# GpSimd's last two column sums wait for VectorE, the sum over rows moves to other PSUM banks, and a split moves ahead of two small steps

## The chip, the cores and the metric

The kernel runs on one core of a Trainium2 chip. A core has TensorE (PE in the profile: matmuls; PEld: its weight loads), VectorE (DVE), ScalarE (ACT), GpSimd (POOL) and SyncE (SP, which issues most DMAs). The metric is the device time of one execution in microseconds; three executions of the kernel before took 457.15, 457.48 and 458.14 us, so the time before is the median, 457.48 us.

## The reference

```python
x = A_x                                    # (1, 2048, 512)
g = sigmoid((x * gate_w).sum(-1, keepdims=True))
# a: linear attention, 32 heads of 16
q, k, v = split_heads(x @ wqkv)
pq, pk = q @ w_phi, k @ w_phi              # per head, 16 x 16
phi_q = concat(softmax(pq), softmax(-pq)); phi_k = concat(softmax(pk), softmax(-pk))
kv = phi_k^T v;  z = phi_k.sum over rows
o  = (phi_q kv) / (phi_q . z + 1e-6)
a  = merge_heads(o) @ wo
# b: dense, Mish, dense (512 -> 1376 -> 512)
h = x @ w1 + b1;  b = (h * tanh(softplus(h))) @ w2
return g * a + (1 - g) * b
```

All data is fp32. Matmuls are made of three passes over a rounded high part and a low part of each operand (high x high, high x low, low x high), so most operands have a pair of tiles, h and l, and a step that makes the low part by a subtraction.

## The kernel before, in words

**Stage A** goes over the rows in eight chunks of 256 (two tiles of 128 rows each). For a chunk, TensorE projects k, v and q; the q projection is written to DRAM (`pqd`) for later. For each k tile VectorE makes the arguments of both softmaxes (steps `mx`, `mn`, `d0`, `d1`), ScalarE takes the exponential in place (`E`), VectorE sums per head, inverts and scales (`S`, `rS`, `ml`), TensorE adds phi_k^T v into one PSUM bank (`kv`), and GpSimd adds the tile into `zacc`, 128 x 1024 (`z0`, `z1`, L318). Beside that the weights of b are loaded and split.

**The seam** is the last chunk (the text `LAST`, L55 to 58) and the start of block 0. It also starts block 0: it splits block 0's x into `xbh` (`XH0`, `XH1`, ScalarE) and `xbl` (`XL0`, `XL1`, VectorE, L403), and takes the feature steps of block 0's first two q tiles (names with `+`, which mean the next stage). `zacc` is split into `zs` high (`zh`, ScalarE, L443) and low (`zl`, VectorE, L466), and TensorE multiplies both with a matrix of ones (`z`, L457 to 463), so that every row of `zb` holds the sum over all rows. `km` masks the kv sums, `kt` transposes them into `kvb`.

**Stage B** goes over the rows in four blocks of 512. TensorE works on the dense part: `up0` to `up10` (12 matmuls each, in the order xbh x w1 high, xbh x w1 low, xbl x w1 high), ScalarE takes Mish and makes the high part (`mi`, `hi`), GpSimd the low part (`lo`, L498), and `dn` adds into four PSUM banks (the four row tiles). Between these lie the attention steps: for each of the block's four q tiles, feature steps as above, then the product with `zb` (`T`), its sums (`D`), the denominator (`m`, `de`, `rd`, `sc`), the scaled features (`es`), a 32 x 32 transpose (`tr`); for each pair of tiles 16 DMAs that rearrange the transposed features (`mv`, `tt` into `eT`, L586), the numerator on TensorE (`nu`, 32 matmuls), its split (`oh` on ScalarE, `ol` on VectorE, L607), and the output projection (`wo`, 12 matmuls a tile) with its gated copy (`ag`). `fi` mixes both and stores.

**What sets the order.** Each engine runs its instructions in the order in which the program emits them: `pin` is `tc.keep_in_program_order`, and nearly every instruction is pinned to the one before it on its engine. The order is written out by hand in the texts `FIRST` to `BLOCK` (L39 to 86): words are steps, registered with `at` and called by `run`; a step with `@` in front is one of `mid_ops`, `'` means the previous chunk and `+` the next one. Waits between engines follow from the tiles that are read, written or reused. In `LAST`, before the change, z0 stands ahead of ve0 and of the feature steps of block 0's second q tile; in `BLOCK0`, the row `S1+ T1+ rS1+ D1+ LX0 LX1 nu1 oh1 ol1` puts the reciprocal and the sums of the next block's second tile ahead of ol1 on VectorE. LX0 and LX1 load the next block's x.

PSUM has eight banks: tag `a` has three (projections, `up`, kvT, z, half of num and wo), `dn` four (v, `down`), `kv` one.

The listing has the functions that the diff touches, with the line numbers of the profile.

Of the kernel before, what the change touches and what calls it, by code (L numbers as in the profile page):

```python
# [10 lines left out]
F32R = mybir.dt.float32r  # L11
AF = mybir.ActivationFunctionType
# [3 lines left out]
P = 128  # L16
S = 2048
D = 512
H = 32
DH = 16  # L20
KT = D // P
NG = 4
SC = 256
NCH = S // SC
# [28 lines left out]
    S1 rS1 ml1 z1 v1 ve1 q0 mx0+ mn0+ d00+ d10+ qe0 st0 q1 qe1 st1 E0+ lq1+  # L53
"""
LAST = """  # L55
    k0 mx0 mn0 d00 d10 k1 E0 XH0 kv' mx1 mn1 d01 d11 E1 v0 S0 rS0 ml0 z0 ve0 ldo XH1 mx1+ mn1+ d01+ d11+ E1+
    S1 rS1 ml1 z1 XL0 XL1 v1 ve1 lq2+ q0 WH0 qe0 st0 q1 WH1 zh qe1 st1 zl kv S0+ rS0+ km
"""


# [4 lines left out]
    up4 mi4 hi4 lo4 dn2 E2 S2 T2 rS2 D2 m2 de2 rd2 sc2 es2 tr2 up5 mi5 hi5 lo5 dn3 E3 ge gg up6 mi6 hi6 lo6 dn4  # L65
    up7 mi7 hi7 lo7 dn5 nu0 oh0 S3 T3 rS3 ol0 D3 m3 de3 rd3 sc3 es3 tr3 mv1 up8 mi8 hi8 lo8 dn6
    mx0+ mn0+ d00+ d10+ mx1+ mn1+ d01+ d11+ lq2+ lq3+ wo0 ag0 wo1 ag1 E0+ E1+ S0+ T0+ rS0+ D0+ m0+ de0+ rd0+ sc0+ es0+ tr0+
    up9 mi9 hi9 lo9 dn7 up10 mi10 hi10 lo10 dn8 S1+ T1+ rS1+ D1+ LX0 LX1 nu1 oh1 ol1 m1+ de1+ rd1+ sc1+ es1+ tr1+ mv0+
    XH0+ XL0+ XH1+ XL1+ dn9 wo2 ag2 wo3 ag3 df0 fi0 df1 fi1 df2 fi2 df3 fi3
"""  # L70
BLOCK1 = """
# [18 lines left out]
def tile_gated_mix(ctx: ExitStack, tc: tile.TileContext, xT, wv, wkT, wqT, bd, w1a, w1b, b1, w2a, w2b, wo, out):  # L90
# [6 lines left out]
    pin = tc.keep_in_program_order  # L97
    V, G_, A_, Sy = nc.vector, nc.gpsimd, nc.scalar, nc.sync
# [11 lines left out]
    def k4(name, tag, dt=F32):  # L110
        return T([P, 1024], dt, tag, {"E": 4, "tx": 2, "oh": 2, "z": 1}[tag], name)
# [4 lines left out]
    def psum(name, tag, bufs={"a": 3, "dn": 4, "kv": 1}):  # L116
        nm[0] += 1
        return pp.tile([P, 512], F32, name=f"{name}_{nm[0]}", tag=tag, bufs=bufs[tag])

    def act(out_, in_, fn=AF.Copy, **k):  # L120
        return pin(A_.activation(out_, in_, fn, **k))  # L121

    def kt(t, f):
        return t[:, : KT * f].rearrange("p (k f) -> p k f", f=f)

    def hv(ap):
        return ap.rearrange("p (h f) -> p h f", f=DH)

    def f32(ap):
        return ap.bitcast(F32)  # L130
# [5 lines left out]
    def stage(wT):  # L136
        return T([P, NFA * 512], F32, "w1a", 2, "wT")[:, : KT * 512].rearrange("p (k g f) -> p k g f", k=KT, f=P)

    skT, sqT = stage(wkT), stage(wqT)
    bds = k2("bds", "io")[:, :].rearrange("p (g f) -> p g f", g=NG)  # L140
    pin(A_.dma_start(bds, bd))
# [28 lines left out]
    ps = psum("warm", "dn")  # L170
# [25 lines left out]
    def at(key, name, fn):  # L196
        steps.setdefault((key, name), []).append(fn)
# [12 lines left out]
    zacc = k4("zacc", "z")  # L210
# [39 lines left out]
    def feat_ops(key, t, src, d):  # L250

        n = str(t)

        def red(name, op):
            d[name] = T([P, H], F32, name, 2, name)
            pin(V.tensor_reduce(d[name], hv(src()), axis=AX.X, op=op))  # L256

        def dd(a):
            if "E" not in d:
                d["E"] = k4("E", "E")  # L260
            E = hv(d["E"][:, a * 512 : (a + 1) * 512])
            if a == 0:
                pin(V.tensor_sub(E, hv(src()), d["mx"][:, :, None].to_broadcast([P, H, DH])))
            else:
                pin(V.tensor_sub(E, d["mn"][:, :, None].to_broadcast([P, H, DH]), hv(src())))  # L265

        def ss():
            d["S"] = T([P, 2 * H], F32, "Sm", 2, "Sm")
            pin(V.tensor_reduce(d["S"], hv(d["E"][:, :]), axis=AX.X, op=ALU.add))  # L269

        at(key, "mx" + n, lambda: red("mx", ALU.max))
        at(key, "mn" + n, lambda: red("mn", ALU.min))
        at(key, "d0" + n, lambda: dd(0))
        at(key, "d1" + n, lambda: dd(1))
        at(key, "E" + n, lambda: act(d["E"], d["E"], AF.Exp))
        at(key, "S" + n, ss)
        at(key, "rS" + n, lambda: pin(V.reciprocal(d["S"], d["S"])))  # L277
# [4 lines left out]
    def a_ops(c):  # L282
        key = ("A", c)
        P_ = psA[c] = {}
        for t in range(2):
            d = {}
            Es[c, t] = d

            def k_(t=t):
                P_["k", t] = proj(xs[c], t, wkh, wkl, "a")  # L290

            def v_(t=t):
                P_["v", t] = proj(xs[c], t, wvh, wvl, "dn" if c or t else "kv")

            def q_(t=t):
                P_["q", t] = proj(xs[c], t, wqh, wql, "a")

            def ve(t=t):
                vs[c, t] = k2("v", "io")
                act(vs[c, t], P_["v", t])  # L300

            def qe(t=t):
                P_["qs", t] = k2("qs", "pq")
                act(P_["qs", t], P_["q", t])

            def st(t=t):
                i = 2 * c + t
                pin(Sy.dma_start(pqd[i * P : (i + 1) * P, :], P_["qs", t]))

            at(key, f"k{t}", k_)  # L310
            at(key, f"v{t}", v_)
            at(key, f"q{t}", q_)
            at(key, f"ve{t}", ve)
            at(key, f"qe{t}", qe)
            at(key, f"st{t}", st)
            feat_ops(key, t, lambda t=t: P_["k", t][:, :], d)
            at(key, f"ml{t}", lambda d=d: scale_by(d, V))
            at(key, f"z{t}", lambda d=d: pin(G_.tensor_add(zacc, zacc, d["E"])))  # L318

        def kv():  # L320
            if not kvs:
                kvs.append(psum("kvp", "kv")[:, : NG * 64].rearrange("p (g f) -> p g f", g=NG))
            (kvp,) = kvs
            for t in range(2):
                E, v = Es[c, t]["E"], vs[c, t]
                Ev = E[:, :].rearrange("p (a r b x) -> p b r a x", a=2, r=2, b=8)
                for u in range(8):
                    for r in range(2):
                        o = (u % 2) * 64 + 32 * r
                        mm(kvp[o : o + 32, u // 2, :], v[:, u * 64 + 32 * r : u * 64 + 32 * r + 32], Ev[:, u, r, :, :],  # L330
                           start=(c == 0 and t == 0 and u < 2), stop=(c == NCH - 1 and t == 1), skip_group_check=True)

        at(key, "kv", kv)
        if c + 1 < NCH:
            def xh():
                new_x(c + 1)
                for j in range(2):
                    x_hi(c + 1, j)

            at(key, "xh", xh)  # L340
            for j in range(2):
                at(key, "xl", lambda j=j: x_lo(c + 1, j, G_))
        if c + 2 < NCH:
            at(key, "ldx", lambda: ldx(c + 2))
# [40 lines left out]
    xb = {}  # L385
    wob = {}

    def x_ops(b, load, split):

        raw = {}  # L390
        for h in range(2):
            def ld(h=h):
                raw[h] = k4("xraw", "tx")
                pin(Sy.dma_start(kt(raw[h], SC), xT[2 * b + h]))

            def xh(h=h):
                if b not in xb:
                    xb[b] = kt(k8("xbh", "xbh"), RB), kt(k8("xbl", "xbl"), RB)
                act(xb[b][0][:, :, h * SC : (h + 1) * SC], kt(raw[h], SC))

            def xl(h=h):
                sl = slice(h * SC, (h + 1) * SC)
                pin(V.tensor_sub(xb[b][1][:, :, sl], kt(raw[h], SC), f32(xb[b][0][:, :, sl])))  # L403

            at(load[0], load[1 + h], ld)
            at(split, f"XH{h}", xh)
            at(split, f"XL{h}", xl)
# [28 lines left out]
    B = {}  # L436

    def mid_ops():
        key = ("A", NCH - 1)

        def zh():
            B["zs"] = [k4("zs", "tx", F32R) for _ in range(2)]
            act(B["zs"][0], zacc)  # L443

        def km():
            B["km"] = k2("km", "io")
            shape = [P, NG, 2, 64]
            m = mask[:, :, :, :].rearrange("p r a f -> p r (a f)")[:, None, :, :].to_broadcast(shape)
            pin(V.tensor_mul(B["km"][:, :].rearrange("p (g r f) -> p g r f", g=NG, r=2), kvs[0][:, :, None, :].to_broadcast(shape), m))

        def kt_():
            pt = psum("kvT", "a")
            for G in range(NG):
                pin(nc.tensor.transpose(pt[:, G * P : (G + 1) * P], B["km"][:, G * P : (G + 1) * P], ident))
            act(kvb, pt[:, :].rearrange("p (g d) -> p g d", g=NG))

        def z():  # L457
            B["zb"] = k4("zb", "z")
            for a in range(2):
                ps = psum("z", "a")  # L460
                for j in range(2):
                    mm(ps, onr, B["zs"][j][:, a * 512 : (a + 1) * 512], start=(j == 0), stop=(j == 1))
                act(B["zb"][:, a * 512 : (a + 1) * 512], ps)

        at(key, "zh", zh)
        at(key, "zl", lambda: pin(V.tensor_sub(B["zs"][1], zacc, f32(B["zs"][0]))))  # L466
        at(key, "km", km)
        at(("B", 0), "@kt", kt_)
        at(("B", 0), "@z", z)


# [302 lines left out]
```

## Time and profile before

| | |
|---|---|
| runs | 457.15, 457.48 (median), 458.14 us |
| profiled execution, first to last instruction (span) | 455.6 us |
| profiled execution, own device time | not given apart from its span |
| granted TensorE clock | 0.998 of full speed |

The profile is of one execution. Its timeline has, per row, the start and the duration in us, the engine, the line, the operation, and output tile <- input tiles with partitions x elements; `x4` means that four such instructions are merged into the row. What stands in brackets is how long the engine stood idle before it, and what released it. L101 and L121 are the helpers through which all matmuls and all activations go, so these are told apart by their tiles. In the view of waits a row has the waiting engine, tile and line, whom it waited for, and then total us, number of waits and the longest. The chain of waits is followed back from the last instruction; its rows have start, duration and what ran. SPq is SyncE's DMA queue.

### The profile page before, as it was taken

Reading aid. Unit: us, or ns where it says so; the run is one execution under the profiler, and the core shown is the slowest. Engines: PE = TensorE matmul, PEld = TensorE weight load, DVE = VectorE, ACT = ScalarE, POOL = GpSimd, SP = SyncE. Lnnn points to the kernel's source line nnn. Section 1 sums busy time; section 2 is a strip of 40 time slices with the busy share of each in tenths; the row PEclk is TensorE's granted clock in tenths of the full one; section 3 lists DMA queues with packets and bytes.
Section 4 is the critical chain, followed back from the end, with each engine's and each line's share of the span. In section 5 each row is a group of like instructions: output and inputs, shape, how many; then the busy total and the mean of one; then the engine's idle time right before and its main releaser. Section 6 shows DMA issues by size and latency. Waiting matters only on the chain.

```text
span 455.6 us, 6980 instructions
## 1 busy us (share of the span) xinstructions
PE 445.6 (98%) x2772; PEld 363.4 (80%) x2772; DVE 306.8 (67%) x402; ACT 195.0 (43%) x265; POOL 161.4 (35%) x102
## 2 busy tenths in 40 slices
PE   7999999999999899999899999999999999999996
PEld 6888888888888678878687887887887888787885
DVE  2599459369399999799987985666967629611002
ACT  3554443443334645726337354434254553234220
POOL 3338777767862355221123212023212122221211
PEclk9999999999999999999999999999999999999999
DMA  7721513505523110313434050332041402030002
GB/s 284 247 83 56 168 53 129 186 8 179 183 82 106 47 23 2 94 46 86 146 94 138 17 158 14 108 115 54 23 119 53 112 19 94 1 81 13 1 1 92
DMA packets 25593, 40.07 MB, mean 88 GB/s; under 512 B 5716, under 2 KB 13908, under 8 KB 25560
## 3 DMA queue, kind: packets, MB, share of 16 engines
q1 hardware_dynamic: 25384, 39.35, 28.4%
q8 instruction: 22, 0.36, 0.3%
q10 hardware_dynamic: 144, 0.26, 0.2%
q14 instruction: 11, 0.09, 0.1%
q0 software_dynamic: 32, 0.01, 0.0%
HBM read 22.82 MB, written 8.40 MB: 69 GB/s over the span
## 4 chain that ended last, share of the span: by engine, by line
PE 61%; DVE 4%; ACT 1%; issue 0%
PE up L101 25%; PE down L101 24%; PE wo L101 10%; PE num L101 2%; DVE xbl L403 1%; DVE Sm L269 1%; DVE T L548 0%; DVE Dn L552 0%; DVE io L633 0%; ACT L121 0%; DVE tt L566 0%; DVE E L280 0%; DVE Dn L572 0%; ACT E L121 0%; DVE Sm L277 0%; ACT io L121 0%
## 5 line engine op out<-in xcount | busy, mean ns | idle before, releaser
L498 POOL TENSOR_TENSOR l<-act,h 128x512 fp32r<-128x512 f32 x44 | 60.7, 1380 | 224.2 <-ACT h L121 189.4
L121 ACT ACTIVATE act<-up,b1s 128x512 f32<-128x512 f32 x44 | 30.3, 689 | 91.5 <-PE up L101 90.3
L318 POOL TENSOR_TENSOR zacc<-zacc,E 128x1024 f32<-128x1024 f32 x16 | 39.7, 2482 | 45.8 <-DVE E L280 31.4
L121 ACT ACTIVATE E<-E 128x1024 f32<-128x1024 f32 x32 | 33.6, 1059 | 49.4 <-DVE E L265 49.4
L280 DVE TENSOR_TENSOR E<-E,Sm 128x1024 f32<-128x1024 f32 x32 | 44.0, 1375 | 1.1
L101 PE MATMUL wo<-woh,ohl 128*128 128x512 f32 x128 | 40.8, 390 | 1.2 <-DVE ohl L607 1.2
L269 DVE TENSOR_REDUCE Sm<-E 128x64 f32<-128x1024 f32 x32 | 38.7, 1209 | 3.8 <-ACT E L121 3.8
L101 PE MATMUL down<-w2ah,h 128*128 128x512 f32 x96 | 37.5, 390 | 0.0
L101 PE MATMUL down<-w2al,h 128*128 128x512 f32 x96 | 37.4, 389 | 0.0
L101 PE MATMUL down<-w2ah,l 128*128 128x512 f32 x96 | 37.4, 389 | 0.0
L633 DVE SCALAR_TENSOR_TENSOR io<-down,og_sb,io 128x512 f32<-128x512 f32 x16 | 11.3, 751 | 31.1 <-PE down L101 31.0
L256 DVE TENSOR_REDUCE mx<-proj 128x32 f32<-128x512 f32 x16 | 11.0, 689 | 30.8 <-PE proj L101 30.8
L101 PE MATMUL down<-w2bh,h 128*128 128x512 f32 x80 | 31.2, 391 | 0.0
L101 PE MATMUL down<-w2bl,h 128*128 128x512 f32 x80 | 31.1, 389 | 0.0
L101 PE MATMUL down<-w2bh,l 128*128 128x512 f32 x80 | 31.1, 389 | 0.0
L101 PEld LDWEIGHTS wo<-woh,ohl 128*128 128x128 f32 x128 | 24.0, 188 | 6.6 <-DVE ohl L607 1.6
L121 ACT ACT_TABLE_LOAD x19 | 24.4, 1283 | 10.1 <-PE up L101 9.8
L121 ACT ACTIVATE h<-act 128x512 fp32r<-128x512 f32 x44 | 27.8, 632 | 1.4
L607 DVE TENSOR_TENSOR ohl<-num,ohl 128x512 fp32r<-128x512 f32 x16 | 10.2, 678 | 26.4 <-ACT ohl L121 26.4
L101 PE MATMUL up<-xbl,w1ah 128*128 128x512 f32 x96 | 25.8, 391 | 1.5 <-DVE xbl L403 1.5
L101 PE MATMUL up<-xbh,w1ah 128*128 128x512 f32 x96 | 26.3, 396 | 0.2 <-ACT zb L121 0.2
L101 PE MATMUL up<-xbh,w1al 128*128 128x512 f32 x96 | 25.7, 389 | 0.0
(113 smaller groups left out, 970.6 us busy)
## 6 DMA issues: line engine op xcount, KB each, us to landing
xraw<-in_xT_dram SPq DMA_DIRECT2D x16, 512.0 KB, 4.8
eT<-tt SPq DMA_DIRECT2D x128, 64.0 KB, 2.0
pqd<-qs SPq DMA_DIRECT2D x16, 256.0 KB, 3.5
pq<-pqd SPq DMA_DIRECT2D x16, 256.0 KB, 2.8
out_dram<-io SPq DMA_DIRECT2D x16, 256.0 KB, 2.1
raw<-in_w1a_dram SPq DMA_DIRECT2D x3, 512.0 KB, 3.6
raw<-in_w2a_dram SPq DMA_DIRECT2D x3, 512.0 KB, 3.7
wT<-in_wkT_dram SPq DMA_DIRECT2D x4, 256.0 KB, 5.4
```

What stands on the lines that cost most here:

```text
L101: return pin(nc.tensor.matmul(*a, **k))
L121: return pin(A_.activation(out_, in_, fn, **k))
L256: pin(V.tensor_reduce(d[name], hv(src()), axis=AX.X, op=op))
L269: pin(V.tensor_reduce(d["S"], hv(d["E"][:, :]), axis=AX.X, op=ALU.add))
L280: pin(eng.tensor_mul(hv(d["E"][:, :]), hv(d["E"][:, :]), d["S"][:, :, None].to_broadcast([P, 2 * H, DH])))
L318: at(key, f"z{t}", lambda d=d: pin(G_.tensor_add(zacc, zacc, d["E"])))
L403: pin(V.tensor_sub(xb[b][1][:, :, sl], kt(raw[h], SC), f32(xb[b][0][:, :, sl])))
L498: pin(G_.tensor_sub(U[i]["l"], U[i]["a"], f32(U[i]["h"])))
L607: pin(V.tensor_sub(ohl[h, gp][:, 512:], num[h, gp], f32(ohl[h, gp][:, :512])))
L633: pin(V.scalar_tensor_tensor(io[t], dn[t], og_sb[:, i : i + 1], io[t], op0=ALU.mult, op1=ALU.add))
```

## The change

1. In `LAST`, z0 moves behind `d11+` and z1 behind `XL1`. The first GpSimd instruction of each also gets a hand-made dependency: z0 on the subtraction of d11+, z1 on that of XL1 (`last[0]` and `last[1]`). z1 is made of two halves of 512 columns.
2. `zh` and `zl` are in halves as well (`zh0 zl0 zh1 zl1`), and stand at the end of `LAST`, behind `km`.
3. A step `tb` asks for the activation table of Mish, behind `qe1 st1`. It isn't pinned.
4. z's two PSUM tiles are taken from tag `dn` instead of `a`.
5. In `BLOCK0`, `nu1 oh1 ol1` move ahead of `rS1+ D1+ LX0 LX1`.

```diff
 LAST
-    k0 mx0 mn0 d00 d10 k1 E0 XH0 kv' mx1 mn1 d01 d11 E1 v0 S0 rS0 ml0 z0 ve0 ldo XH1 mx1+ mn1+ d01+ d11+ E1+
-    S1 rS1 ml1 z1 XL0 XL1 v1 ve1 lq2+ q0 WH0 qe0 st0 q1 WH1 zh qe1 st1 zl kv S0+ rS0+ km
+    k0 mx0 mn0 d00 d10 k1 E0 XH0 kv' mx1 mn1 d01 d11 E1 v0 S0 rS0 ml0 ve0 ldo XH1 mx1+ mn1+ d01+ d11+ z0 E1+
+    S1 rS1 ml1 XL0 XL1 z1 v1 ve1 lq2+ q0 WH0 qe0 st0 q1 WH1 qe1 st1 tb kv S0+ rS0+ km zh0 zl0 zh1 zl1
 BLOCK0
-    up9 mi9 hi9 lo9 dn7 up10 mi10 hi10 lo10 dn8 S1+ T1+ rS1+ D1+ LX0 LX1 nu1 oh1 ol1 m1+ de1+ rd1+ sc1+ es1+ tr1+ mv0+
+    up9 mi9 hi9 lo9 dn7 up10 mi10 hi10 lo10 dn8 S1+ T1+ nu1 oh1 ol1 rS1+ D1+ LX0 LX1 m1+ de1+ rd1+ sc1+ es1+ tr1+ mv0+
...
+    SYNC = mybir.DependencyInfo(mybir.DependencyClass.Sync, mybir.DependencyReason.DATA)
+    last = {}
...
-                pin(V.tensor_sub(E, d["mn"][:, :, None].to_broadcast([P, H, DH]), hv(src())))
+                ins = pin(V.tensor_sub(E, d["mn"][:, :, None].to_broadcast([P, H, DH]), hv(src())))
+                if key == ("B", 0) and t == 1:
+                    last[0] = ins
...
-            at(key, f"z{t}", lambda d=d: pin(G_.tensor_add(zacc, zacc, d["E"])))
+            def zs(t=t, d=d):
+                for a in range(2 if c == NCH - 1 and t else 1):
+                    sl = slice(a * 512, a * 512 + 512) if c == NCH - 1 and t else slice(0, 1024)
+                    ins = pin(G_.tensor_add(zacc[:, sl], zacc[:, sl], d["E"][:, sl]))
+                    if c == NCH - 1 and not a:
+                        tc.add_manual_dep(ins.ins, last[t].ins.name, SYNC, reason="VectorE's own sums first")
+            at(key, f"z{t}", zs)
...
-                pin(V.tensor_sub(xb[b][1][:, :, sl], kt(raw[h], SC), f32(xb[b][0][:, :, sl])))
+                last[h] = pin(V.tensor_sub(xb[b][1][:, :, sl], kt(raw[h], SC), f32(xb[b][0][:, :, sl])))
...
-        def zh():
-            B["zs"] = [k4("zs", "tx", F32R) for _ in range(2)]
-            act(B["zs"][0], zacc)
+        def zh(a):
+            if not a:
+                B["zs"] = [k4("zs", "tx", F32R) for _ in range(2)]
+            sl = slice(a * 512, a * 512 + 512)
+            act(B["zs"][0][:, sl], zacc[:, sl])
+        def zl(a):
+            sl = slice(a * 512, a * 512 + 512)
+            pin(V.tensor_sub(B["zs"][1][:, sl], zacc[:, sl], f32(B["zs"][0][:, sl])))
...
-                ps = psum("z", "a")
+                ps = psum("z", "dn")
...
-        at(key, "zh", zh)
-        at(key, "zl", lambda: pin(V.tensor_sub(B["zs"][1], zacc, f32(B["zs"][0]))))
+        for a in range(2):
+            at(key, f"zh{a}", lambda a=a: zh(a))
+            at(key, f"zl{a}", lambda a=a: zl(a))
+        at(key, "tb", lambda: A_.preload_act_table(AF.Mish))
```

## The prediction

> **What bounds the kernel now.** The page comes first: its first line gives the span, and part 1 says which engine fills it.
>
> ```profile
> span 455.6 us, 6980 instructions
> PE 445.6 (98%) x2772; PEld 363.4 (80%) x2772; DVE 306.8 (67%) x402; ACT 195.0 (43%) x265; POOL 161.4 (35%) x102
> ```
>
> TensorE (PE) is busy for 98%. A change elsewhere pays only where TensorE waits, so the second view is the waits of TensorE alone, from 140 us (just ahead of the seam) to the end:
>
> ```profile
> PE up L101 <- DVE xbl L403: 1.5, 1, 1.5
> PE wo L101 <- DVE ohl L607: 1.2, 1, 1.2
> PE up L101 <- ACT zb L121: 0.2, 1, 0.2
> ```
>
> Three single waits, two at the seam and one late in block 0. The third view is the timeline around them, with one piece of the chain of work for the pace.
>
> ```profile
> 154.37 1.07 PE L101 MATMUL up<-xbh,w1al 128*128 128x512 f32 x4
> 156.95 1.20 PE L101 MATMUL up<-xbl,w1ah 128*128 128x512 f32 x4 [1.51 <-DVE xbl L403]
> 160.74 1.07 PE L101 MATMUL z<-zs,onr 128*128 128x512 f32 x4
> 162.04 1.20 PE L101 MATMUL up<-xbh,w1ah 128*128 128x512 f32 x4 [0.23 <-ACT zb L121]
> ...
> 222.05 0.39 PE L101 MATMUL down<-w2bh,l 128*128 128x512 f32 x1
> 223.63 0.50 PE L101 MATMUL wo<-woh,ohl 128*128 128x512 f32 x1 [1.20 <-DVE ohl L607]
> ```
> ```profile
> 167.77 2.72 PE up L101 x12
> ...
> 232.09 8.16 PE up L101 x36
> ```
>
> Twelve matmuls in 2.72 us are 0.227 each, 0.91 for four; a group of four is shown 1.07 long because ends overlap, and 1.20 after a stall, so restarting costs 0.13. What each stall truly takes:
> - xbl: unstalled, the group after 154.37 would start at 155.28. It starts at 156.95: 1.67 + 0.13 = 1.80 us.
> - zb: the group after 160.74 would start at 161.65, not 162.04: 0.39 + 0.13 = 0.52.
> - wo: the matmul after 222.05 would start at 222.28, not 223.63: 1.35, plus 0.50 - 0.39 = 0.11 for the restart, 1.46.
>
> Together 3.78 us. That is all the change can win, since TensorE waits for nothing else there.
>
> **The change part by part.** Why is xbl late? VectorE (DVE) and GpSimd (POOL) at the seam:
>
> ```profile
> 145.91 2.40 POOL L318 TENSOR_TENSOR zacc<-zacc,E 128x1024 f32<-128x1024 f32 x1 [8.80 <-ACT xbh L121]
> 146.25 0.67 DVE L256 TENSOR_REDUCE mn<-pq 128x32 f32<-128x512 f32 x1
> 146.85 2.01 DVE L263 TENSOR_TENSOR E<-pq,mx 128x512 f32<-128x512 f32 x1
> 148.78 0.68 DVE L265 TENSOR_TENSOR E<-mn,pq 128x512 f32<-128x512 f32 x1
> 149.38 1.21 DVE L269 TENSOR_REDUCE Sm<-E 128x64 f32<-128x1024 f32 x1
> 150.62 0.55 DVE L277 RECIPROCAL Sm<-Sm 128x64 f32<-128x64 f32 x1
> 151.21 1.22 DVE L280 TENSOR_TENSOR E<-E,Sm 128x1024 f32<-128x1024 f32 x1
> 152.35 4.55 DVE L403 TENSOR_TENSOR xbl<-xraw,xbh 128x1024 fp32r<-128x1024 f32 x2
> ...
> 152.60 3.21 POOL L318 TENSOR_TENSOR zacc<-zacc,E 128x1024 f32<-128x1024 f32 x1 [4.29 <-ACT qs L121]
> ```
> ```profile
> 129.59 2.39 POOL L318 TENSOR_TENSOR zacc<-zacc,E 128x1024 f32<-128x1024 f32 x1 [5.54 <-DVE E L280]
> 131.17 1.89 DVE L280 TENSOR_TENSOR E<-E,Sm 128x1024 f32<-128x1024 f32 x1
> 227.64 2.32 DVE L403 TENSOR_TENSOR xbl<-xraw,xbh 128x1024 fp32r<-128x1024 f32 x2
> ```
>
> Undisturbed, the pair of xbl steps takes 2.32 (227.64, in block 0); here 4.55, ending at 156.90, which is 1.09 after the sum z1 ends (152.60 + 3.21 = 155.81). In the same way d01+ (146.85) ends 0.55 after z0 (148.31), and the scaling at 131.17 ends 1.08 after GpSimd's step (131.98). Each looks like a VectorE step that stood still until GpSimd was done and then ran its own length. The reduce that ran wholly beside z0 (mn1, 0.67) was not stretched.
>
> The Trainium skill states this as a lock ("SBUF — State Buffer", Who interferes with whom): a VectorE instruction with two SBUF inputs and a GpSimd one that reads SBUF exclude each other, whoever starts first holding it throughout. The trace agrees (ends 1.09, 0.55 and 1.08 after GpSimd's). The rule speaks partly against this change: moved behind d11+, z0 meets ml1, which also reads two SBUF tiles, so one loss is exchanged for another; without the lock ml1 would end near 151.1, with it 0.7 later, which comes out of the cover below and not out of the sum.
>
> *Sums moved.* Without z0 beside it, d01+ takes 0.68, so d11+ ends 1.33 earlier, near 148.13 (149.46 - 1.33). z0 starts 0.17 after its releaser, 148.30, as z1 started 0.17 after ml1's end (152.43), and ends at 150.70. S1 and rS1 run beside it; ml1, ready at 149.88, waits and ends 1.08 after z0: 151.78 (152.43 before). The xbl pair starts 0.08 ahead of that, as now, and ends at 151.70 + 2.32 = 154.02. TensorE needs it at 155.28: **the 1.80 goes, with 1.2 in hand.** Behind z0 GpSimd has only z1 and lo0 queued; z1 waited for ml1 anyway.
>
> *z in halves.* What is late next is zs.
>
> ```profile
> 152.42 1.06 ACT L121 ACTIVATE woh<-raw 128x1024 fp32r<-128x1024 f32 x1
> 155.85 1.06 ACT L121 ACTIVATE zs<-zacc 128x1024 fp32r<-128x1024 f32 x1 [2.37 <-POOL zacc L318]
> 156.81 0.58 ACT L121 ACTIVATE qs<-proj 128x512 f32<-128x512 f32 x1
> 157.41 1.28 ACT L121 ACT_TABLE_LOAD   x1
> ...
> 159.85 0.63 DVE L449 TENSOR_TENSOR km<-kvp,mask 128x512 f32<-128x512 f32 x1
> 160.13 1.29 POOL L498 TENSOR_TENSOR l<-act,h 128x512 fp32r<-128x512 f32 x1 [4.32 <-ACT h L121]
> 160.40 1.21 DVE L269 TENSOR_REDUCE Sm<-E 128x64 f32<-128x1024 f32 x1
> ```
>
> A half sum by lo0's row is 1.29 (two take 0.18 more than one whole, 2.40). z1's halves run from 154.02 + 0.17 = 154.19 to 156.77. VectorE meanwhile does S0+, rS0+ and km (1.2 + 0.5 + 0.6, to 156.3); zl0 then stands behind the second half until 156.77 and ends near 157.3. ScalarE (ACT) ends the last weight copy at 153.48, qs at 154.1, the moved table load at 155.4, zh0 at 156.1, zh1 (0.63) at 157.4, so zl1 ends at 158.05. TensorE, unstalled, ends up1 at 155.28 + 0.91 + 2.72 = 158.91 and then wants zs: **0.86 in hand.** The next reduce, S1, starts at 158.0 instead of 160.40: VectorE comes 2.4 earlier.
>
> *z in down's banks.* up2 no longer needs the bank that zb empties, so the 0.52 goes. zb then ends near 160.7; dn0, the next user of those banks, comes at 158.91 + 0.91 + 2.72 = 162.54. Cover 1.8. Without it the 0.52 returns.
>
> *Table load (tb).* It is not kept in program order, so where it lands is open. Where it is written it lies in ScalarE's gap. If the load stays in front of mi0, mi0 starts at 158.7 as now, lo0 ends about 161.4 as now (160.13 + 1.29), still ahead of 162.54: 0. If it falls between two Exps, it brings a second load, 2 x 1.28 = 2.6 on an engine that is busy for 43%. Bounds 0 to +2.6, below nothing excluded because TensorE has no further wait to lose; I take 0, as ScalarE's own gap at 153.5 is 2.4 long.
>
> *num's low part first.* In block 0:
>
> ```profile
> 181.98 10.25 SPq L586 DMA_DIRECT2D eT<-tt  x16
> 193.87 1.25 DVE L566 STREAM_TRANSPOSE tt<-E 128x1024 f32<-128x1024 f32 x1 [2.84 <-DMA eT<-tt]
> 205.87 10.18 SPq L586 DMA_DIRECT2D eT<-tt  x16
> ...
> 210.73 1.22 DVE L269 TENSOR_REDUCE Sm<-E 128x64 f32<-128x1024 f32 x1 [0.18 <-ACT E L121]
> ...
> 218.40 1.09 PE L101 MATMUL num<-eT,kvb 64*32 64x256 f32 x32
> ...
> 221.36 0.55 DVE L277 RECIPROCAL Sm<-Sm 128x64 f32<-128x64 f32 x1
> 221.82 1.16 DVE L552 TENSOR_REDUCE Dn<-T 128x64 f32<-128x1024 f32 x1
> 222.90 1.27 DVE L607 TENSOR_TENSOR ohl<-num,ohl 128x512 fp32r<-128x512 f32 x2
> ```
>
> ol1 stood behind the reciprocal and the reduce; it now starts at 221.36 instead of 222.90, 1.54 earlier, and wo, which started 0.73 after it, could start at 222.09, ahead of 222.28. **The 1.46 goes, with 0.19 in hand**, if VectorE has moved as far as TensorE. LX1 is issued about 1.2 later in VectorE's time, by one ol1 pair; block 1's split of x ended at 229.96 (227.64 + 2.32) and is first wanted by the ninth matmul of up0, 232.09 + 8 x 0.227 = 233.9: 3.9 of cover, enough for the 1.2 and for TensorE's 1.46 together.
>
> *Does VectorE follow?* TensorE enters block 0 2.32 earlier. VectorE must too: eT's transfers take 193.87 - 181.98 = 11.9, so the second lot lands at 205.87 + 11.9 = 217.8, only 0.6 ahead of num (218.40). VectorE starts 2.4 earlier and meets GpSimd's lo steps, which follow TensorE's clock, as now. I take 2.3 for both. Downstream nothing waits. Sum: 1.80 + 0.52 + 1.46 = 3.78. The profiled span of 455.6 becomes 451.8; some 1.9 lies outside it, as the median of the runs is 457.48: **453.7 us**.
>
> **Rivals.**
> - *VectorE does not follow.* If locks in block 0 give back its 2.3, S0+ (210.73) starts at about 210.5, ol1 10.6 later, wo at 221.8: 1.8 won, 455.7. For: VectorE is nearly gapless there (from 195 to 224 us it waited 0.18, at 210.73), so what it loses it keeps. Against: it meets the same GpSimd steps, moved alike. By the lock rule of that page (who starts first wins) a near tie can fall the other way than before, which is how this rival would come about; no row of before can show such a turn.
> - *GpSimd is not what holds xbl.* Then xbl ends at 156.90 still, the sums start at 157.07, zs is ready near 161.0: 0.3 late at z, 0.52 won, wo 1.46: about 455.9. Against: three ends agree.
> - *Slower.* VectorE loses two more encounters with 1,024-wide GpSimd steps (2.39 each, 129.59) in block 0 between S1 and the first eT transfers: 4.8 against 2.3 won, 2.5 later than now. num and then wo wait for it: 457.48 - 1.8 + 2.5 = 458.2. It decides from 1.8 of lateness on. Against: only two such steps lie there (WL0, WL1), and they already collide.
> - *The table load lands between Exps.* Up to 2.6 back on ScalarE, hidden or not: 453.7 to 456.3.
>
> **How the numbers follow.** The full sum 0.62 (453.0 to 454.3, the runs spreading by 1.0); VectorE or ScalarE giving back part, to 455.7, 0.17; the xbl theory wrong 0.08; most given back, within 0.2% of 457.48 (0.9 us, about what can be told from no change), 0.07; slower by more 0.06. Faster is 0.62 + 0.17 + 0.08 = 0.87. The range 453.0 to 456.0 holds the first three.
>
> **What would show it.** In the changed profile: TensorE's waits for xbl, zb and ohl gone; the xbl pair at 2.3; z0 ending ahead of ml1 and stretching it to about 1.9; z at 158.9 with no wait for zs; the first eT transfers near 179.7; wo2 directly behind down. A TensorE wait for eT or ohl would mean that VectorE lagged; a wait of z for zs that the halves came late; two table loads more than before that tb fell among the Exps.

## The result, and the profile after

The changed kernel takes 454.04 us (median of 6 runs, 452.39 to 454.64), beside 457.08 for the kernel before in the same comparison (456.67 to 458.14): a ratio of 0.9923, with a 95% interval of 0.991 to 0.9937, or 2.9 to 4.1 us less. The profiled execution took 452.97 us with a span of 451.3.

The span and the engines' busy times from the changed kernel's page, then all the waits of TensorE in it:

```profile
span 451.3 us, 6983 instructions
PE 444.3 (98%) x2772; PEld 363.2 (80%) x2772; DVE 304.2 (67%) x403; ACT 197.6 (44%) x268; POOL 160.3 (36%) x103
```
```profile
PE fuse L101 <- DMA bds<-in_bd_dram: 1.9, 1, 1.9
PE warm L101 <- DVE ones L171: 1.1, 1, 1.1
```

All three waits behind 140 us are gone. What is left is at the head, in the first 6 us. The timeline of the seam, to be laid beside the rows in the prediction (lines of the code have moved: L403 is now L415, L318 is L326, L466 is L461, L607 is L627, L586 is L606, L566 is L586):

```profile
146.30 0.68 DVE L265 TENSOR_TENSOR E<-pq,mx 128x512 f32<-128x512 f32 x1
147.75 2.41 POOL L326 TENSOR_TENSOR zacc<-zacc,E 128x1024 f32<-128x1024 f32 x1 [11.19 <-DVE E L267]
149.34 1.91 DVE L284 TENSOR_TENSOR E<-E,Sm 128x1024 f32<-128x1024 f32 x1
151.17 2.35 DVE L415 TENSOR_TENSOR xbl<-xraw,xbh 128x1024 fp32r<-128x1024 f32 x2
152.79 1.20 PE L101 MATMUL up<-xbh,w1ah 128*128 128x512 f32 x4
153.66 2.55 POOL L326 TENSOR_TENSOR zacc<-zacc,E 128x512 f32<-128x512 f32 x2 [3.50 <-DVE xbl L415]
...
156.89 1.28 ACT L121 ACT_TABLE_LOAD   x1
156.91 0.69 DVE L461 TENSOR_TENSOR zs<-zacc,zs 128x512 fp32r<-128x512 f32 x1 [0.15 <-ACT zs L121]
157.52 1.22 DVE L273 TENSOR_REDUCE Sm<-E 128x64 f32<-128x1024 f32 x1
158.36 1.07 PE L101 MATMUL z<-zs,onr 128*128 128x512 f32 x4
159.27 1.07 PE L101 MATMUL up<-xbh,w1ah 128*128 128x512 f32 x4
```

d0 of block 0's second tile takes 0.68 instead of 2.01, the xbl pair 2.35 instead of 4.55; z0 now stretches ml1 (1.91) instead; z and up2 start in step with no bracket. The same kernel in block 0:

```profile
179.08 10.26 SPq L606 DMA_DIRECT2D eT<-tt  x16
190.94 1.25 DVE L586 STREAM_TRANSPOSE tt<-E 128x1024 f32<-128x1024 f32 x1 [2.81 <-DMA eT<-tt]
202.97 10.18 SPq L606 DMA_DIRECT2D eT<-tt  x16
207.83 1.22 DVE L273 TENSOR_REDUCE Sm<-E 128x64 f32<-128x1024 f32 x1 [0.18 <-ACT E L121]
215.50 1.09 PE L101 MATMUL num<-eT,kvb 64*32 64x256 f32 x32
218.47 1.28 DVE L627 TENSOR_TENSOR ohl<-num,ohl 128x512 fp32r<-128x512 f32 x2
219.15 0.40 PE L101 MATMUL down<-w2bh,l 128*128 128x512 f32 x1
219.38 0.40 PE L101 MATMUL wo<-woh,ohl 128*128 128x512 f32 x1
```

wo follows down after 0.23, one matmul's pace.

**A clock for comparing.** The span fell by 4.3, but up0 of block 0 also starts 0.55 earlier (152.79 against 153.34), by differences in the first 13 us. The only step of the change that ran there is `tb`, at 2.86, and the next step of ScalarE (at 8.10) waited for TensorE all the same. Over all the kernels below but the last, whose load at the head is cut, this start lies between 152.24 and 154.00. So each profile is read from the start of up0 to the end of the span. That is 455.6 - 153.34 = 302.26 before and 298.51 after: 3.75 less. Each kernel has one profile. The five kernels in which TensorE waits for nothing behind the head (the change, tb pinned, sums whole, one more tr1, bds in four) lie between 298.38 and 298.59, so a difference of 0.2 on this clock means nothing.

| kernel | up0 starts | span | from up0 to the end | against before |
|---|---|---|---|---|
| before | 153.34 | 455.6 | 302.26 | |
| the change | 152.79 | 451.3 | 298.51 | -3.75 |
| low part alone | 152.33 | 453.1 | 300.77 | -1.49 |
| seam alone | 153.09 | 453.0 | 299.91 | -2.35 |
| before, last sums left out | 153.63 | 454.1 | 300.47 | -1.79 |
| the change, tb pinned | 153.22 | 451.6 | 298.38 | -3.88 |
| the change, z in tag a | 153.46 | 453.6 | 300.14 | -2.12 |
| the same, tb pinned | 153.35 | 452.3 | 298.95 | -3.31 |
| the change, sums back | 154.00 | 453.2 | 299.20 | -3.06 |
| the change, sums whole | 153.53 | 452.0 | 298.47 | -3.79 |
| before, memsets for z1 | 153.35 | 453.8 | 300.45 | -1.81 |
| the change, one more tr1 | 152.24 | 450.7 | 298.46 | -3.80 |
| the change, three more tr1 | 152.71 | 453.4 | 300.69 | -1.57 |
| tb pinned, bds in four | 156.01 | 454.6 | 298.59 | -3.67 |

### The profile page after: what moved, and what is told of

Same layout as the page of the kernel before. It is cut to its first block, busy times and chain, and to the rows that moved or that the text cites. A ratio compares the mean times of both kernels' runs of the same rounds, so it can differ in the third digit from the quotient of the medians.

```text
span 451.3 us, 6983 instructions
## 1 busy us (share of the span) xinstructions
PE 444.3 (98%) x2772; PEld 363.2 (80%) x2772; DVE 304.2 (67%) x403; ACT 197.6 (44%) x268; POOL 160.3 (36%) x103
## 4 chain that ended last, share of the span: by engine, by line
PE 98%; DMA 1%; DVE 0%; issue 0%
PE proj L101 29%; PE up L101 27%; PE down L101 26%; PE wo L101 10%; PE num L101 2%; PE kvp L101 2%; PE fuse L101 2%; DMA bds<-in_bd_dram 1%; DVE io L653 0%; PE z L101 0%; PE kvT L472 0%
## 5 line engine op out<-in xcount | busy, mean ns | idle before, releaser
L326 POOL TENSOR_TENSOR zacc<-zacc,E 128x1024 f32<-128x1024 f32 (+1 forms) x17 | 39.1, 2301 | 47.4 <-DVE E L284 31.4
L627 DVE TENSOR_TENSOR ohl<-num,ohl 128x512 fp32r<-128x512 f32 x16 | 10.2, 678 | 26.3 <-ACT ohl L121 26.3
```

The source lines that it names most:

```text
L326: ins = pin(G_.tensor_add(zacc[:, sl], zacc[:, sl], d["E"][:, sl]))
L627: pin(V.tensor_sub(ohl[h, gp][:, 512:], num[h, gp], f32(ohl[h, gp][:, :512])))
```

## The experiments

The theory: TensorE's three waits were the whole price, and the first came from GpSimd's sums, beside which VectorE's steps that read two SBUF tiles stand still. The rivals: VectorE's chain sets block 0 by itself, or something else stretches xbl.

### The low part alone, and the seam alone

```diff
 low part alone: before, with
-    ... S1+ T1+ rS1+ D1+ LX0 LX1 nu1 oh1 ol1 m1+ ...
+    ... S1+ T1+ nu1 oh1 ol1 rS1+ D1+ LX0 LX1 m1+ ...
 seam alone: the change, with this line as before
```

> The kernel before with part 5 alone: nu1 oh1 ol1 ahead of rS1+ D1+ LX0 LX1. Theory (TensorE's three waits are the whole of it): the wait of wo for ohl goes and the waits for xbl (1.5) and zb (0.2) stay, so 1.46 us less than before: 455.6 from 457.08. Rival (VectorE's chain sets the end of block 0 by itself): wo still waits, or num waits for eT instead; 0 to 0.5 us less.

> The change without part 5: ol1 behind rS1+ and D1+ again. Theory: no wait of TensorE at the seam, and the wait of wo for ohl is back at 1.2, since VectorE comes as much earlier as TensorE does: 2.32 us less than before, 1.46 more than the whole change: about 455.0 to 455.5. Rival (VectorE does not follow TensorE): the wait for ohl grows by what VectorE lags, up to 2.3 us, and nothing is won on before.

The low part alone took 455.93 us (456.89 before; ratio 0.9984, 0.9974 to 0.9995), the seam alone 455.42 (0.9967, 0.9954 to 0.998). From up0 they win 1.49 and 2.35, together 3.84, where the whole change wins 3.75; 1.46 and 2.32 were expected. The medians of the runs, which hold the head as well, give less: 0.96 and 1.47, with intervals of 0.2 to 1.2 and 0.9 to 2.1, and both leave out what was expected. up0's start differs by up to 1.8 between the kernels, so the head can hide as much, but that it does so here is not shown. TensorE's waits behind 140 us, first with the low part alone, then with the seam alone:

```profile
PE up L101 <- DVE xbl L403: 1.5, 1, 1.5
...
PE up L101 <- ACT zb L121: 0.2, 1, 0.2
```
```profile
PE wo L101 <- DVE ohl L627: 1.2, 1, 1.2
```

Each part removes its own wait and leaves the others at their old length, so the parts add up on the clock from up0, and in the second kernel VectorE had moved as far as TensorE: the wait for ohl didn't grow.

### The last two sums left out

```diff
-    ... S0 rS0 ml0 z0 ve0 ...   S1 rS1 ml1 z1 XL0 XL1 ...
+    ... S0 rS0 ml0 ve0 ...      S1 rS1 ml1 XL0 XL1 ...
```

> The kernel before, with GpSimd's last two sums left out (zacc lacks the last 256 rows). Theory (GpSimd's sums hold VectorE's steps with two inputs in SBUF): the subtraction d0 of block 0's second tile takes 0.68 instead of 2.01, the xbl pair 2.3 instead of 4.55, TensorE does not wait for xbl (1.8 less), the short wait for zb stays: 455.3. Rival (something else stretches the xbl pair, the DMAs or ScalarE's copies beside it): the pair stays at 4.5 and the time at 457.1.

455.18 us (0.9964, 0.9952 to 0.9975); 1.79 less from up0.

```profile
147.14 0.68 DVE L263 TENSOR_TENSOR E<-pq,mx 128x512 f32<-128x512 f32 x1
...
151.31 2.35 DVE L404 TENSOR_TENSOR xbl<-xraw,xbh 128x1024 fp32r<-128x1024 f32 x2
```

With GpSimd's sums gone and all DMAs and copies in place, both steps have their own length. The rival that something else stretches xbl falls.

### The sums back in their old places, z1 in halves

```diff
 the change, with
-    ml0 ve0 ldo XH1 mx1+ mn1+ d01+ d11+ z0 E1+   S1 rS1 ml1 XL0 XL1 z1
+    ml0 z0 ve0 ldo XH1 mx1+ mn1+ d01+ d11+ E1+   S1 rS1 ml1 z1 XL0 XL1
-                    if c == NCH - 1 and not a:
-                        tc.add_manual_dep(...)
```

> The change with both GpSimd sums where they stood before and without the two added waits; z1 still in halves, zh and zl late. Theory (each side stands still until the other's instruction is over, and the one that waits goes next): d0 of block 0's second tile takes 2.0 again; xbl's first half runs, then z1's first half, then xbl's second half: the pair takes about 3.5 instead of 2.35, ending 0.6 after TensorE wants it, and the time from up0's start grows by 0.75 to 299.25. Rival (the two share bandwidth in proportion): the pair takes 4.5 as before and 1.8 come back: 300.3.

453.80 us (0.9927, 0.9906 to 0.9948); 0.69 more from up0 than the change (299.20, where 299.25 was expected). That rests on one profile of each; the runs don't tell this kernel from the change, whose ratio is 0.9923.

```profile
153.01 3.45 DVE L413 TENSOR_TENSOR xbl<-xraw,xbh 128x1024 fp32r<-128x1024 f32 x2
153.27 4.35 POOL L326 TENSOR_TENSOR zacc<-zacc,E 128x512 f32<-128x512 f32 x2 [4.30 <-ACT qs L121]
```

The pair takes 3.45: xbl gives way to one half sum of 1.3 and not to the whole one of 2.4. Two halves of the sum take 4.35 instead of 2.55, since they stand still for one xbl half each. That is taking turns by whole instructions, the side that waited going next; by the rival, sharing in proportion, the pair would have stayed at 4.5. So cutting GpSimd's instruction in two takes 1.1 of the 2.2 off the pair by itself, and the added waits are worth the remaining 0.69 on TensorE. The lock of the Trainium skill ("SBUF — State Buffer", Who interferes with whom), held for a whole instruction, fits the 3.45.

### Memsets in the place of z1

```diff
 before, with, for the last tile of the last chunk,
-            pin(G_.tensor_add(zacc, zacc, d["E"]))
+            for _ in range(3):
+                pin(G_.memset(zacc, 0.0))
```

> The kernel before, with z1 replaced by three memsets of zacc (GpSimd writes SBUF and reads nothing; the sum over rows is lost). Theory (it is GpSimd's reads that stop a VectorE step with two SBUF inputs): the xbl pair takes 2.35 beside them and TensorE does not wait for xbl; from up0's start to the end 300.5. Rival (any GpSimd instruction on SBUF stops it): the pair takes 3 to 4.5 and TensorE waits 0.5 to 1.5.

455.50 us in its one run. Inconclusive for the question as put: the memsets, which wait for no E tile, ran at once behind z0 and were over before xbl. What they did meet was d11+:

```profile
148.38 2.98 POOL L321 MEMSET zacc<- 128x1024 f32 x3
148.80 0.68 DVE L265 TENSOR_TENSOR E<-mn,pq 128x512 f32<-128x512 f32 x1
```

d11+, a VectorE step with two SBUF inputs, kept its 0.68 beside a GpSimd instruction that only writes. The same section of the Trainium skill says so: a step with two SBUF inputs contends with a GpSimd instruction that reads, not with one that only writes. One case here agrees; xbl itself beside a memset wasn't tried again.

### The sums whole

```diff
 the change, with z1, zh and zl of 1,024 columns each
-    S0+ rS0+ km zh0 zl0 zh1 zl1
+    S0+ rS0+ km zh0 zl0
```

> The change with z1, zh and zl whole instead of in halves. Theory (0.86 of cover at z, halves save about that): zs is ready 2.40 + 1.06 + 1.23 after z1's start, 158.4 on the change's clock, where TensorE wants it at 158.4: a wait of 0 to 0.3, and 0 to 0.45 more from up0's start to the end (298.5 to 298.95). Rival (the halves are what makes the seam work): z waits over 0.5.

453.63 us (0.9919, 0.9902 to 0.9935); from up0 298.47, as the change.

```profile
154.40 2.40 POOL L326 TENSOR_TENSOR zacc<-zacc,E 128x1024 f32<-128x1024 f32 x1 [3.50 <-DVE xbl L415]
156.83 1.06 ACT L121 ACTIVATE zs<-zacc 128x1024 fp32r<-128x1024 f32 x1 [3.63 <-POOL zacc L326]
157.92 1.23 DVE L461 TENSOR_TENSOR zs<-zacc,zs 128x1024 fp32r<-128x1024 f32 x1 [1.41 <-ACT zs L121]
159.10 1.09 PE L101 MATMUL z<-zs,onr 128*128 128x512 f32 x4
```

zl ends at 159.15, with z's first matmul at 159.10 (its low part is read by the second): just in time. Behind the added wait the halves bring nothing that can be measured; without it they brought 1.1 on xbl.

### z in tag a, with tb floating and with tb pinned

```diff
 the change, with
-                ps = psum("z", "dn")
+                ps = psum("z", "a")
 tb pinned:
-        at(key, "tb", lambda: A_.preload_act_table(AF.Mish))
+        at(key, "tb", lambda: pin(A_.preload_act_table(AF.Mish)))
```

> The change with z's two tiles in the banks of tag a again. Theory: up2 waits for zb once more (0.2 shown), and from the start of up0 to the end the kernel takes 0.5 us more than the change: 299.0 instead of 298.5 in the profile. Rival (the earlier zs alone removes that wait): no wait and 298.5.

> The change with the table load tb kept in program order. In the changed profile tb ran at 2.9 us, and the load of Mish's table still stood ahead of mi0, at 156.9. Theory (cover): 20 table loads instead of 22, mi0 1.3 earlier, lo0 1.3 earlier, no change of TensorE: the same time as the whole change within 0.3 us. Rival (tb's floating cost or won something at the head or the seam): over 0.5 us of difference in TensorE's start of up0 or z.

> The change with tb pinned and z's tiles in tag a's banks. With z in those banks but tb floating, z's second half waited 1.2 for gr, which stood on ScalarE behind the table load, mi0 and hi0, and the time from up0's start to the end grew by 1.63. Theory (it is the table load in front of mi0 that makes that bank late): with the load out of the way gr ends 1.3 earlier, z waits 0 to 0.15 and up2 0.1 to 0.3 for zb, and from up0's start to the end 298.8 to 299.0. Rival (z in tag a's banks costs this however early ScalarE is): z waits 1.2 again and 300.1.

z in tag a with tb floating took 455.09 us (0.9953, 0.9936 to 0.997), and from up0 1.63 more than the change, not the 0.5 that was expected. The wait stands at another place: z's second half waits for gr, which copies the row of the gate out of up0's bank, the bank that z takes next.

```profile
157.56 1.28 ACT L121 ACT_TABLE_LOAD   x1
158.85 0.69 ACT L121 ACTIVATE act<-up,b1s 128x512 f32<-128x512 f32 x1
159.03 0.61 PE L101 MATMUL z<-zs,onr 128*128 128x512 f32 x2
159.57 0.63 ACT L121 ACTIVATE h<-act 128x512 fp32r<-128x512 f32 x1
160.22 0.59 ACT L121 ACTIVATE gr<-up 1x512 f32<-1x512 f32 x1
...
160.87 0.73 PE L101 MATMUL z<-zs,onr 128*128 128x512 f32 x2 [1.22 <-ACT gr L121]
```

On ScalarE gr stands behind zh1, the table load, mi0 and hi0. tb pinned alone changes nothing: 453.36 us (0.9925, 0.9907 to 0.9943), 298.38 from up0. With both, 454.02 us (0.9942, 0.9922 to 0.9962) and 298.95 from up0: z doesn't wait, and up2 waits 0.2 for zb, as expected; so it was the table load in front of mi0 that made gr too late for z. The bank is worth 1.63 while the load stands in front of mi0, and 0.57 (298.95 - 298.38) where it doesn't, and a working tb is worth something (1.19) only if z's banks are tag a's.

### VectorE late in block 0

```diff
 the change, with n = 1 or 3 more transposes tr1 in block 0
-                pin(V.transpose(...))
+                for _ in range(n + 1 if b == 0 and t == 1 else 1):
+                    pin(V.transpose(...))
```

> The change with one more copy of the transpose tr1 in block 0 (1.17 us of VectorE ahead of the first eT transfers). Theory (VectorE's chain by way of eT stands 0.6 ahead of TensorE at num and 0.2 at wo): num waits about 0.6 for eT, wo about 0.1 to 0.3 for ohl, and from up0's start to the end the kernel takes 0.7 to 0.9 more: 299.2 to 299.4. Rival (VectorE has room in block 0, since TensorE waits for nothing there): nothing more, 298.5.

> The change with three more copies of tr1 (3.51 us of VectorE). Theory: the lateness goes through one for one less the covers: num of the first pair waits near 1.9 for eT, and in all 3.0 to 3.3 more from up0's start to the end: 301.5 to 301.8, which is within 1 us of the kernel before (302.26). Rival (room on VectorE): 298.5 to 299.5.

One more: 452.78 us (0.9917, 0.9897 to 0.9937), 298.46 from up0, nothing lost. The expectation was wrong. Three more: 455.63 (0.9974, 0.9959 to 0.999), 2.18 lost, not 3.0 to 3.3. Two rows of the kernel with one more tr1:

```profile
179.81 10.25 SPq L607 DMA_DIRECT2D eT<-tt  x16
...
202.41 10.18 SPq L607 DMA_DIRECT2D eT<-tt  x16
```

From up0's start, the first eT transfers come at 27.57 instead of 26.29, 1.28 late (1.17 was expected of the copy), but the second at 50.17 instead of 50.18. The lateness was lost in between, at two steps of VectorE that used to stand behind GpSimd's lo steps. The small step on the gate, then the product m3, each with the lo step of GpSimd beside or ahead of it, in the change and below with one more tr1:

```profile
191.43 1.29 POOL L518 TENSOR_TENSOR l<-act,h 128x512 fp32r<-128x512 f32 x1 [2.15 <-issue]
192.11 0.63 DVE L549 TENSOR_SCALAR ge_sb<-ge_sb 128x4 f32<-128x4 f32 x1
...
198.12 1.29 POOL L518 TENSOR_TENSOR l<-act,h 128x512 fp32r<-128x512 f32 x1 [5.39 <-ACT h L121]
198.18 1.31 DVE L592 TENSOR_TENSOR Dn<-Dn,Sm 128x64 f32<-128x64 f32 x1
```
```profile
190.87 1.28 POOL L518 TENSOR_TENSOR l<-act,h 128x512 fp32r<-128x512 f32 x1 [2.40 <-issue]
192.85 0.13 DVE L549 TENSOR_SCALAR ge_sb<-ge_sb 128x4 f32<-128x4 f32 x1
...
197.56 1.29 POOL L518 TENSOR_TENSOR l<-act,h 128x512 fp32r<-128x512 f32 x1 [5.40 <-ACT h L121]
198.41 0.52 DVE L593 TENSOR_TENSOR Dn<-Dn,Sm 128x64 f32<-128x64 f32 x1
```

0.50 and 0.79, together 1.29. VectorE came later, while GpSimd kept to TensorE's clock: at the small step it had ended already (192.15), and at m3 it had 0.44 left instead of 1.23. With three more, the first transfers came at 30.13 (3.84 late) and the second at 52.43 (2.25 late): 1.59 was absorbed, at the same two steps (0.13 and 0.23 long). This much lateness did reach the first num, which waited 1.61 and then took 1.61 instead of 1.09 itself:

```profile
194.10 1.61 PE L101 MATMUL num<-eT,kvb 64*32 64x256 f32 x32 [1.61 <-DMA eT<-tt]
```

So there are two kinds of room. 3.84 of lateness cost 2.18, and that at the first num, which therefore has about 1.7 of its own (an estimate from these two numbers); 1.28 stays within it. The second num has less, about 0.7 in the change: its transfers take 11.9 from 202.97, and it starts at 215.50. By this count the 1.29 that came back was needed there; no kernel here shows the second num without it.

### The load of bds in four

```diff
 tb pinned, with
-    pin(A_.dma_start(bds, bd))
+    for g in range(NG):
+        pin(A_.dma_start(bds[:, g, :], bd[:, g, :]))
```

> The change with tb pinned and the 256 KB load of bds cut into four transfers, one for each group of matmuls. After the change TensorE waits for nothing from 6 us on but for 1.9 for bds at the head. Theory: the first group's 64 KB lands earlier and fuse starts up to 1 us earlier: 0.3 to 1 us less than the change. Rival (the first piece of wT, 256 KB, lands no earlier, and what it frees is waited for there): the same time, up0 starting at 152.3 to 153.6 as in the runs so far.

455.95 us (0.9982, 0.9972 to 0.9992), worse than the change; both theories missed. From up0 it is as fast (298.59), so the loss is at the head: up0 starts at 156.01.

```profile
5.57 0.80 PE L101 MATMUL fuse<-bds,wT 128*128 128x128 f32 x2 [1.52 <-DMA bds<-in_bd_dram]
...
8.11 5.03 PE L101 MATMUL fuse<-bds,wT 128*128 128x128 f32 x20 [0.76 <-DMA bds<-in_bd_dram]
```

The first piece came 0.4 earlier than the whole had in the change (5.99); TensorE's last wait for a piece ended 2 later than that. Why four transfers take longer than one wasn't pursued. No kernel here is shown to beat the change.

## Why the prediction was right, point by point

- **Sums moved (1.80).** Right: the same 1.79 goes when the sums are left out. d01+, z0, ml1 and xbl came as worked out (0.68, 2.41, 1.91, 2.35).
- **z in halves, 0.86 in hand.** zl1 ended at 157.60, z started at 158.36: 0.76. Right in the sum, but with the sums whole the time was the same (298.47), so the halves weren't needed for it.
- **z in down's banks (0.52).** The wait went. As a price of leaving z in tag a it was mis-sized: 1.63, since z itself would have waited for gr behind the table load, a wait that the prediction didn't name. With the load out of the way it is 0.57.
- **tb (0, bounds 0 to 2.6).** It didn't do what it says. It ran at 2.86 us, while ScalarE waited at the head, and the table of Exp had to be loaded again at 22.39; two table loads more, as the last part of the prediction would read, though not among the Exps but ahead of the first:

```profile
2.86 1.28 ACT L486 ACT_TABLE_LOAD   x1
...
22.39 1.28 ACT L121 ACT_TABLE_LOAD   x1
```

  The value taken, 0, held for that place too.
- **num's low part (1.46).** Right: 1.49 alone.
- **VectorE follows.** Right: eT at 179.08, which is 179.63 on the clock of before (0.55 added), where 179.7 was forecast. A near tie such as the rival speaks of did come up. It fell to VectorE: T0 started at 161.97, lo1 at 162.58, and T0 kept its 1.21. With tb pinned it fell to GpSimd (lo1 at 161.85, T0 at 161.99), T0 took 2.32, and still the first eT transfers came 26.29 after up0's start, as in the change. So the rival's premise, that VectorE keeps what it loses there, was wrong: part comes back at later steps, and 1.28 of added work was swallowed without loss.
- **The sum.** 3.78 forecast, 3.75 in the profiles from up0; 453.7 forecast, 454.04 measured. That these two lie so near is in part luck: beside the changed kernel the kernel before took 457.08, not 457.48, so by the medians 3.04 was won, with an interval of 2.9 to 4.1 that holds 3.78. The span came out at 451.3 and not 451.8, which is the head's 0.55.

## What to carry to other kernels

When one engine is busy for 98%, list its single waits, price each by its pace, and ask of each only who stood in front. A step for which that engine waits, and which is longer than its twins elsewhere and ends a fixed time after another engine's instruction, has stood still; give it its turn first, or cut the other's instruction in two. And check in the trace that an instruction runs where it was written: one that waits for nothing can run far ahead of it.

## What the hardware showed that was not expected

- Time lost to turn-taking between VectorE and GpSimd is also room: 1.28 us of extra VectorE work cost nothing (298.46 beside 298.51), since the first num had room of its own and, ahead of the second, the waits behind GpSimd's steps shrank by 1.29.
- The small VectorE step on the gate, with one SBUF input of 128x4, also took 0.63 beside a GpSimd lo step and 0.13 to 0.17 otherwise, while a reduce wholly beside a sum of GpSimd wasn't stretched (mn1, 0.67, in the kernel before).
- One 256 KB transfer cut into four by columns made TensorE's last wait for it end at 8.11 instead of 5.99.
